# A mixture of experts after a convolution on one core: the fixed blocks of experts 1 to 6 go from 256 to 512 rows

## The chip, the core and the metric

The kernel runs on one core of a Trainium2 chip. Its engines work side by side, each through its own queue in order: TensorE (PE in the profile, its weight loads PEld), VectorE (DVE), ScalarE (ACT), GpSimd (POOL, which issues the indirect gathers and scatters) and SyncE (SP, which issues the other transfers). The metric is the time of one execution in microseconds (us).

## The reference

The input `x` has 8 batches of 3584 rows of 192 numbers. A causal convolution of 7 taps with softmax weights, one set for each of 8 heads of 24 columns, comes first. Then every row is a token of a mixture of 8 experts:

```python
skip_score = x @ w_skip
do_compute = skip_score > 0
xc = x[do_compute]
e_idx = argmax(xc @ w_gate, axis=1)
gate_w = softmax(xc @ w_gate)[arange, e_idx]
for e in range(E):                       # E = 8, D = 192, F = 1024
    mask = e_idx == e
    h = maximum(xc[mask] @ w1[e], 0.0)
    y[mask] = gate_w[mask, None] * (h @ w2[e])
out[do_compute] = xc + y
```

So about half of the 28672 tokens go through one expert each, a product with a 192 x 1024 matrix and one with a 1024 x 192 matrix; the others keep the convolution's result.

## The kernel before

**Two phases.** The first phase convolves batch by batch, stores the result in `out`, routes each token and builds lists of token numbers by expert (`sidx`; `sidxa` for the tokens of the first five batches that chose expert 0 or 1). The second phase works through a list of *blocks*. A block is a group of tokens of one expert; 128 tokens are a *column* of the list (`us` is the block's number of columns, one or two). There are 61 blocks: numbers 0 to 7 (the tail, experts 0 and 1 from `sidxa`, while the first phase ends), 8 to 49 (the fixed sequence: "122" for experts 0 and 1, six blocks of two columns for each of experts 2 to 7), and 50 to 60 (dynamic: whatever is left, expert and column read from a table). `NTAIL` is 8.

**The stages of a block.** `gather` fetches its rows from `out` into a row buffer `y` with one indirect transfer per column, `gather_gates` its gates. `prep` takes the largest absolute value of each row (L779), makes a power of two of it (three small DVE steps), scales the row to f16 on ACT (`yt`, L784), puts the rest that f16 lost beside it with two DVE instructions per column (L789), and transposes it into `m` by a transfer (L792). `up` is the first product: for each group of 128 hidden units five passes of a 128 x 128 weight over the block's rows, into a bank of PSUM (`ph`, 512 columns of f32). With 256 rows a bank holds two groups. ACT takes the positive part in f16 (`hh`, L818), DVE the rest (`hl`, L820), and with that the bank is free. `down` is the second product: for each column 8 times a pass of 384 and one of 192 columns into a bank `po` (L850, L853), and then DVE scales it (`yf`, L830), adds it to the row in two steps (`o`, L836) and POOL scatters it to `out` (L839).

**What sets the order.** Every engine's queue is filled in the order in which the Python code runs. In the loop over blocks at L1087, iteration n writes `up(n+1)`, the gates of n+2, the gathers, then `down(n)`. `weave` runs such a stage, which stops once per bank in `up` (after `hh`, ahead of `hl`) and once per column in `down`, and at each stop it writes one step of background work (`bg`) and PU = 2 or PD = 4 steps of `prep` of a later block. `gather` runs up to AHEAD = 5 blocks ahead, `prep` PREP = 3. The background is `split_weights` of the next expert: 7 loads, 7 DVE reductions of 512 columns (L260), one `partition_all_reduce` on POOL (L266) whose result the next DVE step (`pow2_steps`, L309) needs, then 7 pairs of an ACT and a DVE instruction of 512 columns (L279, L290). It must be over when the next expert's first `up` is written: `background(-1)` writes out what is left of it.

**Banks.** `bank` takes the next PSUM pool in turn. From block 8 on the turn for `ph` is over `ps_h` (3 banks), `ps_h2` (2 banks), `ps_h`; that for `po` over `ps_o` (one bank) and `ps_o2` (two). So every second column's sum goes into the one bank of `ps_o`, and a `ph` bank is used again four, five or six banks later:

```python
def bank(pools):
    pools.append(pools.pop(0))
    return pools[-1]
```

Of the kernel before, what the change touches and what calls it, by code (L numbers as in the profile page):

```python
# [17 lines left out]
P = 128  # L18
# [24 lines left out]
REST = "122"  # L43
# [28 lines left out]
PREP = 3  # L72
PREP0 = 3
# [8 lines left out]
def conv_router_moe(ctx: ExitStack, tc: tile.TileContext, x, weight, w_skip, w_gate, w1, w2, out):  # L82
# [662 lines left out]
    def open_row_buffers():  # L745
        for n in range(DEPTH):
            ybuf.append(wk2.tile([P, 2, D], F32, tag=f"y{n}", bufs=1, name=f"y{n}"))
            gbuf.append(wk2.tile([P, 2], F32, tag=f"g{n}", bufs=1, name=f"g{n}"))
            nc.gpsimd.memset(ybuf[n], 0.0)
            nc.gpsimd.memset(gbuf[n], 0.0)  # L750
# [7 lines left out]

    def gather(k, fixed=True):
        k.y = ybuf[k.n % DEPTH]  # L760
        for u in range(k.us):
            rows_apart(nc.gpsimd.indirect_dma_start(  # L762
                out=k.y[:, u, :], out_offset=None, in_=out[0:k.rows, :],
                in_offset=bass.IndirectOffsetOnAxis(ap=k.si[:, u:u + 1], axis=0),
                bounds_check=k.rows - 1, oob_is_err=False), fixed)

    def gather_gates(k):
        k.g = gbuf[k.n % DEPTH]
        for u in range(k.us):
            nc.gpsimd.indirect_dma_start(  # L770
                out=k.g[:, u:u + 1], out_offset=None, in_=gate_dr[0:k.rows, :],
                in_offset=bass.IndirectOffsetOnAxis(ap=k.si[:, u:u + 1], axis=0),
                bounds_check=k.rows - 1, oob_is_err=False)

    def prep(k):

        am = k.am = wk2.tile([P, 2], F32, tag="yam", bufs=6, name=f"yam{k.n}")
        sc = wk2.tile([P, 2], F32, tag="ysc", bufs=3, name=f"ysc{k.n}")
        nc.vector.tensor_reduce(out=am[:, 0:k.us], in_=k.y[:, 0:k.us], axis=AX.X, op=ALU.max, apply_absolute_value=True)  # L779
        yield  # L780
        yield from pow2_steps(am[:, 0:k.us], sc[:, 0:k.us])
        yt = wk2.tile([P, 2, 2 * D], F16, tag="yt", bufs=3, name=f"yt{k.n}")
        for u in range(k.us):
            nc.scalar.activation(yt[:, u, 0:D], k.y[:, u, :], AF.Copy, scale=sc[:, u:u + 1])  # L784
        yield
        k.m = wk2.tile([P, 3, BLK], F16, tag="m", bufs=MBUF, name=f"m{k.n}")
        for u in range(k.us):
            for (a, b_, o) in ((P, D, D), (0, P, D + 64)):
                nc.vector.scalar_tensor_tensor(out=yt[:, u, o:o + b_ - a], in0=k.y[:, u, a:b_],  # L789
                                               scalar=sc[:, u:u + 1], in1=yt[:, u, a:b_],  # L790
                                               op0=ALU.mult, op1=ALU.subtract)
            nc.sync.dma_start_transpose(out=k.m[:, :, u * P:(u + 1) * P], in_=yt[:, u, :])  # L792
            yield

# [10 lines left out]
    def up(k, wt):  # L805
        k.hh = wk3.tile([P, NF, BLK], F16, tag="hh", bufs=2, name=f"hh{k.n}")
        k.hl = wk3.tile([P, NF, BLK], F16, tag="hl", bufs=2, name=f"hl{k.n}")
# [15 lines left out]
    def down(k, wt, fixed=True):  # L823

        wide = k.n >= NTAIL
        o = wk3.tile([P, 2, D], F32, tag="o", bufs=3, name=f"o{k.n}")
        f2 = wk2.tile([P, 2], F32, tag="yf", name=f"yf{k.n}")

        def scale():
            nc.vector.scalar_tensor_tensor(out=f2[:, 0:k.us], in0=k.am[:, 0:k.us], scalar=winv_of(wt),  # L830
                                           in1=k.g[:, 0:k.us], op0=ALU.mult, op1=ALU.mult)

        def finish_rows(u, *parts):
            base = k.y[:, u, :]
            for part in parts:
                nc.vector.scalar_tensor_tensor(out=o[:, u, :], in0=part, scalar=f2[:, u:u + 1], in1=base,  # L836
                                               op0=ALU.mult, op1=ALU.add)
                base = o[:, u, :]
            rows_apart(nc.gpsimd.indirect_dma_start(  # L839
                out=out[0:k.rows, :], out_offset=bass.IndirectOffsetOnAxis(ap=k.si[:, u:u + 1], axis=0),  # L840
                in_=o[:, u, :], in_offset=None, bounds_check=k.rows - 1, oob_is_err=False), fixed)
# [31 lines left out]
    blocks = []  # L873

    def add_block(si, e=None, l=None, rows=NTOK):
        k = Blk()
        k.n, k.e, k.l, k.si, k.rows, k.us = len(blocks), e, l, si, rows, si.shape[1]
        blocks.append(k)
# [10 lines left out]
    for e in range(E):  # L889
        add_blocks(e, REST if e < NA else "2" * NST,  # L890
# [24 lines left out]
    dynw = {}  # L915
# [10 lines left out]
    for b in range(B):  # L926
        if b == B - 1:
            xeven.close()
            wk2 = ctx.enter_context(tc.tile_pool(name="wk2", bufs=2))
            open_row_buffers()  # L930
# [121 lines left out]
    dynw = {}  # L1052
# [25 lines left out]

    routes.append(whole_route(B - 1))
# [7 lines left out]
    for n in range(NBLK):  # L1087
# [3 lines left out]
        if n == NTAIL:  # L1091
# [3 lines left out]
            wk4 = ctx.enter_context(tc.tile_pool(name="wk4", bufs=1))  # L1095
            ph_pools.append(ctx.enter_context(tc.tile_pool(name="ps_h2", bufs=2, space=PSUM)))
# [8 lines left out]
        m = n + PREP + 1  # L1105
        if m < NBLK and blocks[m].l is not None:
            l = blocks[m].l
            dynw[l] = wk4.tile([P, WW], F16, tag="wd", bufs=5, name=f"wd{l}")
            bg.append(dyn_weights(l, dynw[l]))
        while prepped < min(n + PREP + 1, gathered):  # L1110
# [11 lines left out]
        while gathered < min(n + AHEAD + 1, ready):  # L1122
# [8 lines left out]
        if n >= NTAIL + 8 and n % 2 == 0 and (n - NTAIL - 8) // 2 < NDYN:  # L1131
            dyn_lists((n - NTAIL - 8) // 2)
# [4 lines left out]
    with tc.If(left > 0):  # L1137
        fill = wk4.tile([P, E * SPAN // P], I32, tag="fill", bufs=1, name="fill")
# [9 lines left out]
        for e in range(E):  # L1148
            first = nc.values_load(lo_hi[0:1, e:e + 1], min_val=0, max_val=NTOK // BLK)
            last = nc.values_load(lo_hi[0:1, E + e:E + e + 1], min_val=0, max_val=NTOK // BLK)  # L1150
            with tc.For_i(first, last, 1) as i:
                k = Blk()
                k.n, k.rows, k.us = NBLK + e * DEPTH, NTOK, 2
# [3 lines left out]
                wt = wk4.tile([P, WW], F16, tag="wd", bufs=5, name=f"wf{e}")  # L1157
# [32 lines left out]
```

## Time and profile before

| | |
|---|---|
| three runs | 714.67, 716.00, 716.28 us; median 716.0 |
| the profiled execution | 714.31 us, its span 712.5 us, mean granted TensorE clock 0.969 |
| PE, PEld, DVE, ACT, POOL busy | 93%, 75%, 81%, 45%, 56% of the span |
| PE instructions | 5768 matmuls, as many weight loads |
| `up` of two columns | 40 passes of 256 columns, 4.37 us |
| fixed blocks of two columns | one every 8.29 us from 313 us to the end of the fixed sequence |

Times in the profile are us from the start of the span, each row an instruction or several alike that follow each other (x40): start, length, engine, line, operation, output <- input. A length is that of the whole instruction; the next one may start before it ends, so what an instruction takes from its engine is the distance to the next start. POOL's rows are the making of a transfer's list, not the transfer. "Idle before" and "waits" name the engine or transfer whose signal came last.

### The profile page before, as it was taken

The numbers are of one execution on the slowest core, as the hardware profiler recorded it, in microseconds if no ns is written. First come the engines' busy times: TensorE is split into PE (matmuls) and PEld (weight loads), VectorE is DVE, ScalarE is ACT, GpSimd is POOL, SyncE is SP. The second block draws the span as 40 slices with busy tenths as digits, with TensorE's granted clock in tenths as the row PEclk, the third lists the DMA queues.
The fourth block names the chain that finished last, engine by engine and source line by source line (L and its number), as shares of the span: only waits on it lengthen the run. The fifth ranks groups of instructions, "written<-read, shape, count | busy, mean of one in ns | idle before, by whom it ended". The sixth has DMA issues, their size and how long they took to land.

```text
span 712.5 us, 16377 instructions
## 1 busy us (share of the span) xinstructions
PE 666.1 (93%) x5768; PEld 534.8 (75%) x5768; DVE 580.2 (81%) x1533; ACT 319.6 (45%) x654; POOL 399.5 (56%) x435
## 2 busy tenths in 40 slices
PE   4979699699999889999999999999999999999994
PEld 4646476466678889888888888888888888888883
DVE  4428679589899987998998998998998987777762
ACT  3646376367673223354363453543543533343321
POOL 4401020110750556777777777777777777777642
PEclk8998799799999999999999999999999999999997
DMA  7699889989495355466467357367465536999950
GB/s 227 204 263 291 235 235 287 249 202 268 114 224 180 84 128 130 110 163 150 130 171 171 89 168 181 89 159 170 125 181 118 166 84 182 268 315 267 314 171 12
DMA packets 158037, 129.59 MB, mean 182 GB/s; under 512 B 63238, under 2 KB 144904, under 8 KB 157946
## 3 DMA queue, kind: packets, MB, share of 16 engines
q1 hardware_dynamic: 143226, 106.59, 55.5%
q0 software_dynamic: 14720, 21.86, 12.3%
q8 instruction: 47, 0.77, 0.5%
q14 instruction: 44, 0.36, 0.2%
HBM read 69.76 MB, written 48.15 MB: 165 GB/s over the span
## 4 chain that ended last, share of the span: by engine, by line
PE 71%; DVE 13%; DMA 6%; issue 3%; SPq 2%; ACT 2%; POOL 2%; POOLq 0%; DVEq 0%; ACTq 0%
PE ph L815 33%; PE po L850 18%; PE po L853 9%; DMA out_dram<-ys 5%; PE pc L337 3%; DVE ob L617 3%; PE po L865 2%; PE tp L423 2%; SPq L390 2%; DVE oa L606 1%; DVE hl L820 1%; PE pp L350 1%; DMA raw<-in_moe_w_dram 1%; DVE oa L611 1%; DVE yt L789 1%
## 5 line engine op out<-in xcount | busy, mean ns | idle before, releaser
L818 ACT ACTIVATE hh<-ph 128x512 f16<-128x512 f32 x230 | 133.1, 590 | 226.5 <-PE ph L815 210.8
L815 PE MATMUL ph<-m,wt 128*128 128x256 f16 (+1 forms) x2000 | 220.4, 268 | 4.2 <-DVE hl L820 3.1
L815 PEld LDWEIGHTS <-wt 128*128 128x128 f16 x2000 | 188.7, 98 | 27.2 <-issue 5.0
L850 PE MATMUL po<-wt,hh 128*128 128x384 f16 x656 | 167.5, 326 | 0.0
L820 DVE SCALAR_TENSOR_TENSOR hl<-ph,hh 128x512 f16<-128x512 f32 x230 | 155.4, 685 | 11.1 <-ACT hh L818 9.9
L853 PE MATMUL po<-wt,hl 128*128 128x192 f16 x656 | 147.5, 246 | 0.0
L850 PEld LDWEIGHTS <-hh 128*128 128x128 f16 x808 | 78.3, 98 | 39.7
L770 POOL DMA_INDIRECT g<-gate_dr,sidx x82 | 87.4, 1066 | 25.0 <-issue 24.1
L839 POOL DMA_INDIRECT out_dram<-o,sidx x82 | 84.6, 1031 | 25.1 <-issue 6.4
L762 POOL DMA_INDIRECT y<-out_dram,sidx x82 | 83.9, 1023 | 25.3 <-issue 18.6
L853 PEld LDWEIGHTS <-hl 128*128 128x128 f16 x808 | 79.1, 98 | 10.2
L337 PE MATMUL pc<-xs,toep 128*120 128x360 f32 x224 | 82.1, 491 | 0.0
L836 DVE SCALAR_TENSOR_TENSOR o<-po,yf,y 128x192 f32<-128x192 f32 x115 | 47.3, 415 | 42.3 <-PE po L850 34.6
L784 ACT ACTIVATE yt<-y,ysc 128x192 f16<-128x192 f32 x115 | 46.4, 447 | 62.5 <-DVE ysc L314 52.9
L339 ACT COPY ys<-pc 120x720 f32<-120x720 f32 x56 | 42.6, 761 | 58.1 <-PE pc L337 33.5
L789 DVE SCALAR_TENSOR_TENSOR yt<-y,ysc,yt 128x64 f16<-128x64 f32 x230 | 58.3, 313 | 1.8 <-ACT yt L784 1.7
L337 PEld LDWEIGHTS pc<-xs,toep 128*120 128x120 f32 x224 | 38.3, 191 | 15.0 <-issue 2.0
L423 PE MATMUL tp<-ident,ys 120*128 120x120 f32 x240 | 33.1, 283 | 15.4 <-ACT ya L424 15.4
L260 DVE TENSOR_REDUCE am<-raw 128x1 f32<-128x512 f32 x56 | 37.8, 677 | 11.8 <-DMA raw<-in_moe_w_dram 11.5
L423 PEld LDWEIGHTS tp<-ident,ys 120*128 120x128 f32 x240 | 28.0, 149 | 25.7 <-ACT ya L424 17.7
L290 DVE SCALAR_TENSOR_TENSOR wt<-raw,ar,wt 128x512 f16<-128x512 f32 x56 | 41.8, 747 | 5.7 <-ACT wt L279 5.7
L836 DVE SCALAR_TENSOR_TENSOR o<-po,yf,o 128x192 f32<-128x192 f32 x101 | 42.2, 418 | 3.6
(197 smaller groups left out, 958.2 us busy)
## 6 DMA issues: line engine op xcount, KB each, us to landing
wd<-wscr SPq DMA_DIRECT2D x44, 449.0 KB
xs<-in_x_dram SPq DMA_DIRECT2D x6, 2688.0 KB
out_dram<-ys SPq DMA_DIRECT2D x6, 2610.0 KB
wscr<-wt SPq DMA_DIRECT2D x84, 128.0 KB
raw<-in_moe_w_dram SPq DMA_DIRECT2D x32, 192.0 KB
raw<-in_moe_w_dram SPq DMA_DIRECT2D x8, 512.0 KB
raw<-in_moe_w_dram SPq DMA_DIRECT2D x16, 256.0 KB
wscr<-wt SPq DMA_DIRECT2D x14, 256.0 KB
```

Source lines behind the costliest of these rows:

```text
L337: nc.tensor.matmul(pc[0:R, i, 0:n * G], toep[:, h, :], xs[:, c0 + n * i:c0 + n * i + n, h * G:(h + 1) * G], start=True, stop=True)
L423: nc.tensor.transpose(tp[:, u, :], src, ident[0:R, 0:R])
L762: rows_apart(nc.gpsimd.indirect_dma_start(out=k.y[:, u, :], out_offset=None, in_=out[0:k.rows, :], in_offset=bass.IndirectOffsetOnAxis(ap= ...
L770: nc.gpsimd.indirect_dma_start(out=k.g[:, u:u + 1], out_offset=None, in_=gate_dr[0:k.rows, :], in_offset=bass.IndirectOffsetOnAxis(ap=k.si ...
L789: nc.vector.scalar_tensor_tensor(out=yt[:, u, o:o + b_ - a], in0=k.y[:, u, a:b_], scalar=sc[:, u:u + 1], in1=yt[:, u, a:b_], op0=ALU.mult, ...
L815: nc.tensor.matmul(ph[:, f - f0, :], wt[:, o + f * P:o + (f + 1) * P], k.m[:, m, 0:w], start=(n == 0), stop=(n == len(seq) - 1))
L818: nc.scalar.activation(hh, ph, AF.Relu)
L820: nc.vector.scalar_tensor_tensor(out=k.hl[:, f0:f0 + fs, 0:w], in0=ph, scalar=0.0, in1=hh, op0=ALU.max, op1=ALU.subtract)
L836: nc.vector.scalar_tensor_tensor(out=o[:, u, :], in0=part, scalar=f2[:, u:u + 1], in1=base, op0=ALU.mult, op1=ALU.add)
L839: rows_apart(nc.gpsimd.indirect_dma_start(out=out[0:k.rows, :], out_offset=bass.IndirectOffsetOnAxis(ap=k.si[:, u:u + 1], axis=0), in_=o[: ...
L850: nc.tensor.matmul(po, k.hh[:, f, u * P:(u + 1) * P], w2[:, f], start=(f == 0), stop=(f == NF - 1))
L853: nc.tensor.matmul(po[:, 1], k.hl[:, f, u * P:(u + 1) * P], w2[:, f, 0], start=False, stop=False)
```

## The change

The fixed sequence becomes "122" for expert 0, "14" for expert 1, "444" for experts 2 to 6 and six blocks of two for expert 7: 26 blocks in the place of 42, 45 in all. Blocks 12 to 27 have four columns. In `up` of such a block a pass streams 512 columns and a `ph` bank holds one group of hidden units, so that it stops eight times. Row buffers belong to pairs of columns (a block of four takes two; four more of them are opened at block 8 and set to zero by DVE, where POOL does it for the first seven). `prep` does the reduction, the ACT step and the rest for each pair, and the three small steps once for all. The `hh` and `hl` of wide blocks lie in the end of the memory that the dynamic experts' weights use later. `near` limits gathers to three wide blocks ahead and `prep` to two, and holds wide blocks back until block 8. The dynamic blocks' lists are fetched at every block from 14 on, not at every second one from 16 on.

```diff
-REST = "122"
+REST = ("122", "14")
+DEPTH4 = 11
+AHEAD4 = 3
+PREP4 = 2
+LISTS = 6
+NWD = 5
 def prep(k):
-        nc.vector.tensor_reduce(out=am[:, 0:k.us], in_=k.y[:, 0:k.us], axis=AX.X, op=ALU.max, apply_absolute_value=True)
-        yield
+        for i, us, n in pairs(k):
+            nc.vector.tensor_reduce(out=am[:, us], in_=k.y[i][:, 0:n], axis=AX.X, op=ALU.max, apply_absolute_value=True)
+            yield
         yield from pow2_steps(am[:, 0:k.us], sc[:, 0:k.us])
...
+        for i, us, n in pairs(k):
+            yt = wk2.tile([P, 2, 2 * D], F16, tag="yt", bufs=3, name=f"yt{k.n}_{i}")
+            for u in range(n):
+                nc.scalar.activation(yt[:, u, 0:D], k.y[i][:, u, :], AF.Copy, scale=sc[:, 2 * i + u:2 * i + u + 1])
             yield
+            for u in range(n):
...
+                nc.sync.dma_start_transpose(out=k.m[:, :, v * P:(v + 1) * P], in_=yt[:, u, :])
+                yield
 def up(k, wt):
+        if k.us == 4:
+            k.hh, k.hl = hwide[k.n % 2]
     for e in range(E):
-        add_blocks(e, REST if e < NA else "2" * NST,
+        add_blocks(e, REST[e] if e < NA else "2" * NST if e == E - 1 else "4" * (NST // 2),
+    def near(i, n, small, large):
+        if blocks[i].us == 4 and n < NTAIL:
+            return False
+        return i <= n + small and sum(k.us == 4 for k in blocks[n + 1:i + 1]) <= large
...
+            open_row_buffers(wk4, nc.vector, range(DEPTH, DEPTH4))
...
-        while prepped < min(n + PREP + 1, gathered):
+        while prepped < gathered and near(prepped, n, PREP, PREP4):
...
-        while gathered < min(n + AHEAD + 1, ready):
+        while gathered < ready and near(gathered, n, AHEAD, AHEAD4):
             gather(blocks[gathered])
...
-        if n >= NTAIL + 8 and n % 2 == 0 and (n - NTAIL - 8) // 2 < NDYN:
-            dyn_lists((n - NTAIL - 8) // 2)
+        if 0 <= n - NTAIL - LISTS < NDYN:
+            while tables:
+                tail_slot()
+            dyn_lists(n - NTAIL - LISTS)
```

**What moves on the engines.** On PE 640 matmuls and 640 weight loads go. The three places that the prediction speaks of follow, a row per instruction (or several alike, x2), with its line, operation, output <- input; a bracket names the engines or transfer counters for which the row is written to wait (a wait that an earlier row of the queue already made is not written again).

POOL around block 8 before: gates of blocks 9 and 10 (`g`), rows of 12 and 13 (`y`), the scatters of blocks 7 and 8, the reduction over partitions for expert 2's scales (ISA), and the gates of block 11.

```order
L770 DMA g_1890<-gate_dr,sidx 128x1 x2
L762 DMA y_1901<-out_dram,sidx 128x192 x2
L839 DMA out_dram<-o_3706,sidxa 17920x192
L770 DMA g_1894<-gate_dr,sidx 128x1 x2
L762 DMA y_1905<-out_dram,sidx 128x192 x2
L839 DMA out_dram<-o_3854,sidx 28672x192
L266 ISA sc_3938<-ar_3936 128x2
L770 DMA g_1898<-gate_dr,sidx 128x1
```

and after:

```order
L865 DMA out_dram<-o_0_3736,sidxa 17920x192
L783 DMA g_1894<-gate_dr,sidx 128x1 x2
L775 DMA y_1901<-out_dram,sidx 128x192 x2
L775 DMA y_1905<-out_dram,sidx 128x192 x2
L775 DMA y_3749<-out_dram,sidx 128x192 x2
L775 DMA y_3753<-out_dram,sidx 128x192 x2
L865 DMA out_dram<-o_0_3904,sidx 28672x192
L272 ISA sc_3964<-ar_3962 128x2
L783 DMA g_1898<-gate_dr,sidx 128x1
```

The rows of block 12 moved from ahead of block 7's scatter to behind the gates of block 10, and with blocks 12 and 13 twice as wide eight gathers stand in one piece ahead of the scatter of block 8 and the reduction.

PE at the end of a block's second column before (block 19, the last of expert 2 there; `hh`, `hl` are the stationary operands):

```order
L853 LDWEIGHTS hl19_5114
L853 MATMUL po19_1_5372<-wt2_3486,hl19_5114 128x192
L850 LDWEIGHTS hh19_5113
L850 MATMUL po19_1_5372<-wt2_3486,hh19_5113 128x384
L815 LDWEIGHTS wt3_4542 [waits DMAHW5_49]
L815 MATMUL ph21_0_5397<-m21_5174,wt3_4542 128x256 [waits DMAHW4_49]
```

and after, in `down` of block 14 (its `hh` and `hl` lie in `wdall`):

```order
L879 LDWEIGHTS wdall_3765
L879 MATMUL po14_1_4919<-wt2_3486,wdall_3765 128x192
L876 LDWEIGHTS wdall_3765
L876 MATMUL po14_1_4919<-wt2_3486,wdall_3765 128x384
L876 LDWEIGHTS wdall_3765 [waits DVE_49]
L876 MATMUL po14_2_4945<-wt2_3486,wdall_3765 128x384 [waits PE_49]
```

Before, the first product of block 21 followed a second column; now the block's third column follows, and it takes the bank of `ps_o` that the first column filled, so its first weight load waits for DVE.

DVE where an expert changes, before (end of block 18, then block 20, the first of expert 3; `yam`, `ysc` and `yt` belong to the `prep` of block 22):

```order
L836 SCALAR_TENSOR_TENSOR o18_5207<-po18_1_5232,yf18_5208,y4_1897 128x192 [waits PE_49]
L836 SCALAR_TENSOR_TENSOR o18_5207<-po18_1_5232,yf18_5208,o18_5207 128x192 [waits DVE_49]
L779 TENSOR_REDUCE yam22_5279<-y1_1885 128x2 [waits DMASW3_49,DMASW2_49]
L309 TENSOR_SCALAR yam22_5279<-yam22_5279 128x2 [waits DVE_49]
L820 SCALAR_TENSOR_TENSOR hl20_5266<-ph20_0_5267,hh20_5265 128x512 [waits Activation_49]
L311 TENSOR_SCALAR yam22_5279<-yam22_5279 128x2 [waits DVE_49]
L314 TENSOR_SCALAR ysc22_5280<-yam22_5279 128x2 [waits DVE_49]
L820 SCALAR_TENSOR_TENSOR hl20_5266<-ph20_2_5284,hh20_5265 128x512 [waits Activation_49]
L789 SCALAR_TENSOR_TENSOR yt22_5298<-y1_1885,ysc22_5280,yt22_5298 128x64 [waits DMAHW1_49,DMAHW0_49,Activation_49]
```

and after (end of block 14, then block 16, the first of expert 3; the `prep` is that of block 17, and the `hl` of block 16 is written to `wdall`):

```order
L862 SCALAR_TENSOR_TENSOR o14_2_4966<-po14_3_4972,yf14_4889,o14_2_4966 128x192 [waits DVE_49]
L296 SCALAR_TENSOR_TENSOR wt3_4540<-raw3_4548,ar3_4794,wt3_4540 128x512 [waits Activation_49] x3
L793 TENSOR_REDUCE yam17_5028<-y4_1897 128x2 [waits DMASW5_49,DMASW4_49]
L793 TENSOR_REDUCE yam17_5028<-y5_1901 128x2 [waits DMASW7_49,DMASW6_49]
L842 SCALAR_TENSOR_TENSOR wdall_3765<-ph16_0_5021,wdall_3765 128x512 [waits Activation_49]
L315 TENSOR_SCALAR yam17_5028<-yam17_5028 128x4 [waits DVE_49]
L317 TENSOR_SCALAR yam17_5028<-yam17_5028 128x4 [waits DVE_49]
L842 SCALAR_TENSOR_TENSOR wdall_3765<-ph16_1_5033,wdall_3765 128x512 [waits Activation_49]
L320 TENSOR_SCALAR ysc17_5029<-yam17_5028 128x4 [waits DVE_49]
L808 SCALAR_TENSOR_TENSOR yt17_0_5052<-y4_1897,ysc17_5029,yt17_0_5052 128x64 [waits DMAHW7_49,DMAHW6_49,Activation_49]
L808 SCALAR_TENSOR_TENSOR yt17_0_5052<-y4_1897,ysc17_5029,yt17_0_5052 128x128
L842 SCALAR_TENSOR_TENSOR wdall_3765<-ph16_2_5043,wdall_3765 128x512 [waits PE_49]
```

What is left of `split_weights` (three L296 instructions) now stands ahead of block 16's first `hl`, two reductions stand there in the place of one, and the small step that makes `ysc` stands right ahead of the first `yt` that needs ACT's result from it, without an `hl` between.

106 lines of the change are left out of this document (62 added, 44 removed).

## The prediction

> **What bounds the kernel now.** I read the page first, then its span in windows, the waits of PE, the chain of waits, and the timelines of DVE and POOL. The page's busy shares and slices (each digit a fortieth of the span):
>
> ```profile
> PE 666.1 (93%) x5768; PEld 534.8 (75%) x5768; DVE 580.2 (81%) x1533; ACT 319.6 (45%) x654; POOL 399.5 (56%) x435
> PE   4979699699999889999999999999999999999994
> DVE  4428679589899987998998998998998987777762
> PEclk8998799799999999999999999999999999999997
> ```
>
> From the sixteenth slice on PE is full and its clock too; DVE stands at eight or nine tenths until expert 7. The windows of that stretch, busy time with the number of instructions:
>
> ```profile
> core 0: us, PE busy (x) PEld busy (x) DVE busy (x) ACT busy (x) POOL busy (x), PEclk, DMA share, GB/s
> 300.00:360.00 60.00, 60.00 (x544) 49.66 (x542) 56.13 (x162) 28.09 (x56) 46.39 (x46) 1.00 0.57 138
> 600.00:660.00 60.00, 60.00 (x523) 49.07 (x521) 45.37 (x123) 21.69 (x43) 46.27 (x46) 1.00 1.05 279
> ```
>
> PE is the bound, but DVE has only 3.9 us of every 60 left while weights are split. POOL is closer still: 46 instructions, with 0.3 us ahead of each (rows below), make 46.4 + 13.8 = 60.2. The waits of PE from 240 us on, in total, times, longest:
>
> ```profile
> PE ph L815 <- DVE hl L820: 1.8, 1, 1.8
> ```
>
> That one is ahead of the stretch (at 251 us). The chain of waits, merged (start, length), gives the passes:
>
> ```profile
> 292.67 4.37 PE ph L815 x40
> 300.96 2.23 PE ph L815 x40
> 307.11 4.37 PE ph L815 x40
> 313.44 4.37 PE ph L815 x40
> ...
> 404.59 4.37 PE ph L815 x40
> 412.88 4.37 PE ph L815 x40
> ```
>
> Forty passes of 256 columns take 4.37 us, 109.25 ns each; forty of 128 take 2.23, 55.75 each. Two blocks start 8.29 us apart, so a column's second product takes (8.29 - 4.37) / 2 = 1.96.
>
> **The gain.** The two lengths differ by 53.5 ns for 128 columns, so 2.25 ns of each pass do not depend on its columns. 640 passes go: 640 x 2.25 ns = 1.4 us. A wide `up` takes 40 x (55.75 + 3 x 53.5) = 8.65 us, 1.08 per bank. The weight loads that go cost nothing now: they lie beside passes (PEld busy 49.66 of 60, PE never idle). That is all that PE gains; the rest is what the engines behind it must do with blocks twice as long and with no more banks.
>
> **The rule on longer passes.** The Trainium skill (TensorE: Matmul & The Clock Gate, section Back-to-back issue gap) says of streams of load and pass that 128 columns take about 81 ns and 512 about 131. The rows above disagree for 128 columns, 55.75; for 512 no row here shows it, and by the rule the sum would be a large gain; it is the second rival.
>
> **The start of wide blocks.** POOL's timeline around block 8:
>
> ```profile
> 288.16 0.99 POOL L762 DMA_INDIRECT y<-out_dram,sidx  x1 [0.30 <-ACT hh L818]
> ...
> 290.77 1.03 POOL L839 DMA_INDIRECT out_dram<-o,sidxa  x1 [0.30 <-issue]
> 292.10 1.04 POOL L770 DMA_INDIRECT g<-gate_dr,sidx  x1 [0.31 <-issue]
> ...
> 299.61 0.38 POOL L266 PARTITION_ALL_REDUCE sc<-ar  x1 [1.24 <-DVE more L1047]
> ...
> 301.73 1.00 POOL L762 DMA_INDIRECT y<-out_dram,sidx  x1 [0.30 <-issue]
> 303.03 0.99 POOL L762 DMA_INDIRECT y<-out_dram,sidx  x1 [0.30 <-issue]
> ```
>
> A gather takes 1.30 us of the queue, a scatter or gate 1.33. Now block 7's scatter starts at 288.16; two gates, eight gathers and block 8's scatter follow (1.33 + 2.66 + 10.4 + 1.33), so the reduction starts at 303.9 and ends at 304.3, not at 300.0. DVE's timeline shows who needs it:
>
> ```profile
> 301.66 0.16 DVE L309 TENSOR_SCALAR sc<-sc 128x2 f32<-128x2 f32 x1
> ...
> 303.75 0.54 DVE L779 TENSOR_REDUCE yam<-y 128x2 f32<-128x384 f32 x1
> 304.33 0.21 DVE L309 TENSOR_SCALAR yam<-yam 128x2 f32<-128x2 f32 x1
> ...
> 306.06 0.74 DVE L290 SCALAR_TENSOR_TENSOR wt<-raw,ar,wt 128x512 f16<-128x512 f32 x1
> 306.72 1.00 DVE L789 SCALAR_TENSOR_TENSOR yt<-y,ysc,yt 128x64 f16<-128x64 f32 x4
> 307.63 0.22 DVE L830 SCALAR_TENSOR_TENSOR yf<-yam,wt,g 128x2 f32<-128x2 f32 x1
> 307.94 0.42 DVE L836 SCALAR_TENSOR_TENSOR o<-po,yf,y 128x192 f32<-128x192 f32 x1
> 308.39 0.42 DVE L836 SCALAR_TENSOR_TENSOR o<-po,yf,o 128x192 f32<-128x192 f32 x1
> 308.73 0.74 DVE L290 SCALAR_TENSOR_TENSOR wt<-raw,ar,wt 128x512 f16<-128x512 f32 x1
> ...
> 311.49 0.68 DVE L820 SCALAR_TENSOR_TENSOR hl<-ph,hh 128x512 f16<-128x512 f32 x1
> 312.09 0.74 DVE L290 SCALAR_TENSOR_TENSOR wt<-raw,ar,wt 128x512 f16<-128x512 f32 x1
> ```
>
> From start to start: `hl` 0.60, a weight's rest 0.66, a reduction of `y` 0.58, four `yt` 0.91, `yf` 0.31, the two `o` of a column 0.79. The step at 301.66 now waits until 304.35. (The four memsets that DVE takes over cost between nothing and POOL's length; that and the doubled reduction of block 12 lie inside this wait.) From that step to the end of block 12's first `hl` DVE took 312.09 - 301.66 = 10.43 us. After the change that stretch has the second halves of the `prep` of blocks 12 and 13, 0.91 + 0.58 + 0.91, no `prep` of block 14 (0.58 + 0.08 less), and one new wait: `ysc` stands right ahead of the `yt` that goes through ACT. The price of that wait is in three rows of DVE and ACT:
>
> ```profile
> 401.05 0.17 DVE L314 TENSOR_SCALAR ysc<-yam 128x2 int32<-128x2 int32 x1
> ...
> 401.26 0.80 ACT L784 ACTIVATE yt<-y,ysc 128x192 f16<-128x192 f32 x2 [2.13 <-DVE ysc L314]
> ...
> 401.80 1.00 DVE L789 SCALAR_TENSOR_TENSOR yt<-y,ysc,yt 128x64 f16<-128x64 f32 x4
> ```
>
> 0.75 from start to start; an `hl` fills it now, and unfilled it leaves 0.67 idle. So block 12's first `hl` ends at 304.35 + 10.43 + 2.40 - 0.66 + 0.67 = 317.2, its second 1.26 later, 318.45. PE had started this `up` at 307.11. By the turn of the pools its sixth bank is the one that the second `hl` empties (four back), so banks six to eight run from 318.45 to 321.7, where 307.11 + 8.65 = 315.8 was due: 5.9 us lost. Part of it comes earlier, in `down` of block 10, whose second column needs the bank of block 9's second `o`; it is inside the 5.9. The gathers of block 15, which POOL reaches some 10 us late, land while PE is delayed, so they cost nothing; without the delay they would be late next.
>
> **Every change of expert.** Within a wide block the third column takes the bank of the first, so DVE must have its two `o` done 2 x 1.96 us after `up` ends. Count from the start of the `up` at which expert 3's maxima end (block 15; `down` of 14): the last `o` of block 13 0.1 + 0.79, a reduction of weights, two of `y` (1.16), eight `hl` (4.8), another reduction of weights, three small steps and the wait on ACT (0.35 + 0.67), eight `yt` (1.84), the scales (0.5), one rest of weights (0.66), two `yf` (0.62), two `o` (0.79). A weight's reduction is priced by this group of DVE (mean ns of one), less the 0.08 that an `hl` row shows over its step:
>
> ```profile
> L260 DVE TENSOR_REDUCE am<-raw 128x1 f32<-128x512 f32 x35 | 23.7, 677 | 0.2
> ```
>
> Sum 0.89 + 0.6 + 1.16 + 4.8 + 0.6 + 1.02 + 1.84 + 0.5 + 0.66 + 0.62 + 0.79 = 13.5, against 8.65 + 3.92 = 12.57: PE waits 0.9. Then the next block begins at 17.4 with three rests of weights (1.98) and both reductions ahead of its first `hl`; DVE, at 18.3 with the last `o`, reaches the end of the third `hl` at 18.3 + 1.98 + 1.16 + 1.8 + 0.35 + 0.67 + 0.45 = 24.7, and the seventh bank, due at 17.4 + 6 x 1.08 = 23.9, waits 0.8. So 1.7 at each of four changes (2 to 3 up to 5 to 6), and about 1 at expert 6, where the `prep` of a block of two comes on top (1.9 more) without the scales: 7.8 us. Bounds: nothing, if DVE's order leaves the 0.9 and 0.8 as slack; 14, if each of the 15 blocks of experts 2 to 6 lost 0.9. I take 7.8, since it is nearest to DVE's 3.9 us of 60, which is 1.1 in a wide block's 16.5.
>
> **The clock.** The windows ahead of the stretch show what a wait of PE costs beside itself:
>
> ```profile
> core 0: us, PE busy (x), PEclk, DMA share, GB/s
> 248.10:251.50 3.40, 2.82 (x28) 1.00 0.41 87
> 251.30:254.70 3.40, 1.59 (x16) 1.00 0.77 187
> 254.70:258.10 3.40, 3.40 (x24) 0.50 0.35 95
> ```
>
> 0.58 us idle in 3.4 left the clock alone; 1.8 idle were followed by 3.4 us at half clock, a loss of 1.7. PE now waits 3 us and more in `up` of block 12: 1.7 us once, 0 to 3.4 as bounds; the waits of 0.9 are nearer to the 0.58 and cost nothing. The Trainium skill (TensorE: Matmul & The Clock Gate, Part 1: The HAM clock gate) halves the clock after an idle window of about 3.4 us. The trace differs, with 1.8 us of idle time; by the page alone this term could be nothing and the sum 1.7 lower.
>
> **No cost.** The three small steps saved per wide block give DVE 0.3 us, counted above. SP has as many transposes and weight transfers; the dynamic lists move earlier, and no wide block needs them. POOL has as many instructions. The dynamic weights' loads wait for the last wide block, several blocks ahead of use. The end (blocks of two, then dynamic) stays as it is.
>
> **Sum.** 714.3 - 1.4 + 5.9 + 7.8 + 1.7 = 728.3. That is against the profiled execution (714.31 with what lies around its span of 712.5); the median of the runs shown is 1.7 higher and their spread 1.6. I say 729.
>
> **Rivals.** First: DVE is not late. Its waits are spread, and if the stretch to block 12's second `hl` were 5.9 us shorter and the sums at the changes 0.9, PE would keep only its gain: 714.3 - 1.4 = 712.9, faster. For it speaks that PE never waited on DVE in the whole stretch; against it that the same sums leave DVE 1.1 us per wide block on average while a bank must be back after 1.96. Second: a pass of 512 takes far less than two of 256 (the page's rule above). Even then a wide block holds twelve POOL instructions of 1.3 us and more, 15.9 against 16.5, so at most 16 x 0.6 us: 704. Third: only the start is late, the changes fit: 714.3 - 1.4 + 5.9 + 0 to 1.7 = 718.8 to 720.5. For it: the 0.9 and 0.8 are differences of long sums. Fourth: every change of expert halves the clock too: five times 1.7 on top, 737. For it: two waits of 0.9 fall near each other; against: the window with 0.58.
>
> **Chances.** Forecast with its own range 723 to 734: 0.62. Only the start: 0.12. The clock at every change, or more waits of that kind: 0.12. DVE not late: 0.09. Passes cheaper than rows say: 0.01. A net within 0.2% either way, which is about what a measurement of this kernel can tell from no change: 0.04. So faster 0.10, same 0.04, slower 0.86. The range 718 to 740 leaves out the three last cases and little more.
>
> **What would show it.** Right: after 300 us PE's waits name DVE `hl` ahead of `ph` (some 4 us around 315) and DVE `o` ahead of `po`, in groups of one or two per expert; the reduction over partitions starts near 304; a window near 318 has half clock; passes of 512 columns lie 216 ns apart. Wrong: no waits of PE in the wide blocks, or waits for transfers (`m`, `y`), which I priced at nothing, or waits in all of them.

## The result and the profile after

The changed kernel takes 732.04 us (median of 4 runs, 728.88 to 734.8) against 715.34 us for the kernel before (median of 4, 713.56 to 716.28): a ratio on record of 1.0241, 95% interval 1.0211 to 1.0270 (the quotient of the two medians is 1.0233; below it differs from the recorded ratio by up to 0.3%). The ratios leave out executions in a slow state: one of e3_ph5 (1389.52 us) and, with e12_start2, one of each kernel. The forecast was 729, with a range of 718 to 740. The profiled execution took 734.49 us, its span 732.8; it is one of the slower two of the four.

The page of the profiled execution, the lines that answer to those shown of before (busy time and share, then tenths in forty slices):

```profile
PE 666.5 (91%) x5128; PEld 469.5 (64%) x5128; DVE 573.4 (78%) x1493; ACT 319.4 (44%) x654; POOL 396.8 (54%) x435
PE   4979599598998899889999999999998999999995
DVE  4328589589899988996996997987978887777763
PEclk8998799799999999999999999999999999999998
```

PE's busy time is the same, 666.5 us for 666.1: one longer pass in the place of two shorter ones costs nearly what those did. DVE has less to do than before and is still what PE waits for, as the windows (same stretches as before) and PE's waits from 240 to 660 us show (total, times, longest):

```profile
300.00:360.00 60.00, 53.98 (x365) 31.98 (x363) 51.69 (x141) 24.91 (x50) 46.39 (x47) 1.00 0.54 135
600.00:660.00 60.00, 60.00 (x525) 49.38 (x524) 45.38 (x124) 22.34 (x44) 43.76 (x43) 1.00 0.82 225
PE po L876 <- DVE o L862: 8.1, 10, 2.4
PE ph L837 <- DVE wdall L842: 5.2, 7, 1.6
PE inv L595 <- DVE ob L623: 2.3, 3, 1.0
PE ph L837 <- DVE hl L842: 1.8, 1, 1.8
PE ph L837 <- DMA m<-yt: 1.6, 1, 1.6
```

In the wide blocks `hh` and `hl` lie in the tile `wdall`, so the second wait is that on `hl`. The two waits named `inv` and `hl` lie ahead of 300 us. The other three are new and make 14.9 us in all: 5.5 in three waits at the start, 9.4 in fifteen behind it. PE's timeline shows where they stand. Behind the start each of the four changes of expert has a wait of 0.36 on `o` and one of 0.7 on `hl` (372.58 and 383.81, then 425.25 and 436.49). A block ahead of each change stands one more on `o`, of 0.3 to 0.6 (355.57, 408.25), and one of 2.43 stands at the end of expert 6 (times in us from the span's start; the bracket is the idle time ahead of the row and what ended it):

```profile
309.87 0.34 PE L876 MATMUL po<-wt,hh 128*128 128x384 f16 x1 [2.27 <-DVE o L862]
313.58 2.75 PE L837 MATMUL ph<-m,wt 128*128 128x512 f16 x12 [1.57 <-DMA m<-yt]
320.75 3.40 PE L837 MATMUL ph<-m,wt 128*128 128x512 f16 x15 [1.62 <-DVE wdall L842]
325.95 8.80 PE L837 MATMUL ph<-m,wt 128*128 128x512 f16 x40
...
355.57 0.34 PE L876 MATMUL po<-wt,wdall 128*128 128x384 f16 x1 [0.43 <-DVE o L862]
372.58 0.34 PE L876 MATMUL po<-wt,wdall 128*128 128x384 f16 x1 [0.36 <-DVE o L862]
383.81 2.32 PE L837 MATMUL ph<-m,wt 128*128 128x512 f16 x10 [0.67 <-DVE wdall L842]
398.59 3.40 PE L837 MATMUL ph<-m,wt 128*128 128x512 f16 x15 [0.30 <-DVE wdall L842]
402.50 1.24 PE L837 MATMUL ph<-m,wt 128*128 128x512 f16 x5 [0.51 <-DVE wdall L842]
408.25 0.34 PE L876 MATMUL po<-wt,wdall 128*128 128x384 f16 x1 [0.59 <-DVE o L862]
425.25 0.34 PE L876 MATMUL po<-wt,wdall 128*128 128x384 f16 x1 [0.36 <-DVE o L862]
436.49 2.32 PE L837 MATMUL ph<-m,wt 128*128 128x512 f16 x10 [0.67 <-DVE wdall L842]
...
564.83 0.34 PE L876 MATMUL po<-wt,wdall 128*128 128x384 f16 x1 [2.43 <-DVE o L862]
586.91 1.26 PE L837 MATMUL ph<-m,wt 128*128 128x256 f16 x10
```

Forty passes of 512 columns take 8.80 us with the last one's tail, some 216 ns each. A wide block that waits for nothing lasts 16.47 us from one `up` to the next (the one of 325.95 is followed by one at 342.42); two blocks of before last 2 x 8.29 = 16.57.

**A measure that leaves out the early noise.** The first 300 us differ between executions, in a part that the change hardly touches: the last one-column `up` starts between 300.62 and 307.13 us in the profiles of e2 to e10. So the runs below are also compared by the *stretch* from the last one-column `up` (at 302.95 in this profile) to the first `up` of expert 7 (586.91): 284.0 us here. The same stretch takes 269.4 us in the kernel before (from 300.80 to 570.16) and holds one second product of two columns (3.9 us) more there, because blocks of four lag by more columns; 265.4 is therefore what before takes for the same work. 284.0 - 265.4 = 18.6 us are lost. From 325.95 to 586.91 there are 260.96 us for 15 blocks that need 15 x 16.47 = 247.1: 13.9 of the loss lie behind the start.

### The profile page after: what moved, and what is told of

It reads as the page before. It is cut to its first block, busy times and chain, and to the rows that moved or that the text cites. A ratio compares the mean times of both kernels' runs of the same rounds, so it can differ in the third digit from the quotient of the medians.

```text
span 732.8 us, 14932 instructions
## 1 busy us (share of the span) xinstructions
PE 666.5 (91%) x5128; PEld 469.5 (64%) x5128; DVE 573.4 (78%) x1493; ACT 319.4 (44%) x654; POOL 396.8 (54%) x435
## 5 line engine op out<-in xcount | busy, mean ns | idle before, releaser
L837 PE MATMUL ph<-m,wt 128*128 128x512 f16 (+2 forms) x1360 | 217.5, 316 | 11.1 <-DVE wdall L842 5.2
L837 PEld LDWEIGHTS <-wt 128*128 128x128 f16 x1360 | 125.9, 98 | 92.6 <-issue 14.6
L876 PE MATMUL po<-wt,wdall 128*128 128x384 f16 x512 | 131.4, 329 | 5.9 <-DVE o L862 5.8
L840 ACT ACTIVATE wdall<-ph 128x512 f16<-128x512 f32 x128 | 73.6, 590 | 131.9 <-PE ph L837 131.7
L879 PE MATMUL po<-wt,wdall 128*128 128x192 f16 x512 | 115.9, 248 | 0.0
L840 ACT ACTIVATE hh<-ph 128x512 f16<-128x512 f32 x102 | 59.8, 592 | 121.8 <-PE ph L837 120.5
L775 POOL DMA_INDIRECT y<-out_dram,sidx x82 | 82.3, 1004 | 25.3 <-issue 19.8
L842 DVE SCALAR_TENSOR_TENSOR wdall<-ph,wdall 128x512 f16<-128x512 f32 x128 | 85.1, 681 | 0.6 <-ACT wdall L840 0.6
L842 DVE SCALAR_TENSOR_TENSOR hl<-ph,hh 128x512 f16<-128x512 f32 x102 | 69.8, 689 | 9.1 <-ACT hh L840 7.9
L876 PEld LDWEIGHTS <-wdall 128*128 128x128 f16 x512 | 49.9, 99 | 36.1 <-DVE o L862 8.9
L879 PEld LDWEIGHTS <-wdall 128*128 128x128 f16 x512 | 50.5, 99 | 8.6 <-issue 0.3
L266 DVE TENSOR_REDUCE am<-raw 128x1 f32<-128x512 f32 x56 | 37.8, 677 | 14.6 <-DMA raw<-in_moe_w_dram 14.3
L429 PEld LDWEIGHTS tp<-ident,ys 120*128 120x128 f32 x240 | 28.1, 149 | 28.3 <-ACT ya L430 20.1
```

The source lines that it names most:

```text
L429: nc.tensor.transpose(tp[:, u, :], src, ident[0:R, 0:R])
L775: rows_apart(nc.gpsimd.indirect_dma_start(out=row(k, u), out_offset=None, in_=out[0:k.rows, :], in_offset=bass.IndirectOffsetOnAxis(ap=k.s ...
L837: nc.tensor.matmul(ph[:, f - f0, :], wt[:, o + f * P:o + (f + 1) * P], k.m[:, m, 0:w], start=(n == 0), stop=(n == len(seq) - 1))
L840: nc.scalar.activation(hh, ph, AF.Relu)
L842: nc.vector.scalar_tensor_tensor(out=k.hl[:, f0:f0 + fs, 0:w], in0=ph, scalar=0.0, in1=hh, op0=ALU.max, op1=ALU.subtract)
L876: nc.tensor.matmul(po, k.hh[:, f, u * P:(u + 1) * P], w2[:, f], start=(f == 0), stop=(f == NF - 1))
```

## The experiments

Theory A: DVE gives banks back late inside wide blocks, by its order and the few banks. Rivals: what came with the change costs (M); DVE's sheer amount of work (B); `y` reaches DVE late through POOL's queue (Q). All ratios are to the kernel before on the same chip.

| run | edit to the changed kernel | ratio (95%) | stretch, us | PE's waits from 300 to 590 us |
|---|---|---|---|---|
| changed kernel | none | 1.0241 (1.0211 to 1.0270) | 284.0 | 14.9 |
| e1_narrow | blocks of two | 1.0007 (0.9991 to 1.0023) | - | 0.8 |
| e2_po3 | `po` round three banks | 1.0182 (1.0157 to 1.0206) | 277.0 | 10.9 |
| e3_ph5 | `ph` round five banks | 1.0269 (1.0243 to 1.0295) | 284.1 | 14.6 |
| e4_poph | both turns | 1.0140 (1.0115 to 1.0165) | 276.5 | 9.1 |
| e5_start | one wide gather per iteration | 1.0252 (1.0223 to 1.0281) | 285.2 | 15.6 |
| e6_pu1poph | e4, slower `prep` | 1.0064 (1.0039 to 1.0090) | 271.4 | 6.0 |
| e7_gfpoph | e4, `y` ahead of gates | 1.0032 (1.0009 to 1.0055) | 268.9 | 4.0 |
| e8_gfall | e5, e6 and e7 | 1.0077 (1.0050 to 1.0103) | 271.6 | 5.0 |
| e9_gf | `y` ahead of gates alone | 1.0176 (1.0147 to 1.0205) | 277.2 | 11.3 |
| e10_ms | e7, zeroing by ACT | 1.0040 (1.0021 to 1.0059) | 268.7 | 4.0 |

**Blocks of two with all the rest of the change (e1_narrow).**

```diff
-REST = ("122", "14")
+REST = ("122", "122")
-        ... "2" * NST if e == E - 1 else "4" * (NST // 2)
+        ... "2" * NST
```

> All blocks of experts 0 to 7 have two or one column again; the four more row buffers with their memsets on DVE, the early dynamic lists, the shared tile for dynamic weights and the prep code by pairs stay. Theory A (the loss is DVE giving banks back late inside wide blocks): as the kernel before, 713 to 717 us, and PE waits for nothing between 300 and 660 us. Rival M (what came with the change costs: memsets, lists moved earlier, weights in one tile): over 719 us, with waits of PE on m, y or weights.

1.0007 (718.86 us, where the kernel before took 718.66 on that chip), and two waits of 0.4 us, on `o` at 310.19 and on `hl` at 320.14. The buffers, lists and the shared tile cost nothing that the ratio shows and less than 1 us of PE's waits: the loss comes with the wide blocks. Rival M is out.

**The turns of the banks (e2_po3, e3_ph5, e4_poph).**

```diff
             po_pools.append(ctx.enter_context(tc.tile_pool(name="ps_o2", bufs=2, space=PSUM)))
+            po_pools.append(po_pools[-1])                       # e2, e4
-            ph_pools.append(ps_h)
+            ph_pools[:] = [ps_h] * 3 + ph_pools[-1:] * 2        # e3, e4
```

> The changed kernel, but po goes round its three banks (ps_o, ps_o2, ps_o2), so that a column's bank is that of the third column back and not of the second. Theory A (a bank comes back late; DVE has time to spare in the second product, 22.6 us in 31 waits on PE): most of the 8.1 us that PE waits on o go; DVE is then as late as before at the next up, so some of it comes back as waits on hl: 3 to 8 us off, 724 to 729. Rival B (DVE's work is the limit, not the bank's distance): what goes from the waits on o comes back on hl, 732 as the changed kernel.

> The changed kernel, but ph goes round its five banks in the turn 3 + 2, so that each bank comes back five banks later (now four, five or six). Theory A: the 0.7 us waits of up on hl, once per expert, and some 1 us of the one at the start go; the waits on o stay: 2 to 4 us off, 728 to 730. Rival B: 732, the waits on o grow by as much.

> Both turns, of po and of ph, at once. Theory A: a late bank is late for one of the two pools only while the other bridges it, so both together take more than the sum of each: 8 to 11 us off, 721 to 724; what stays is the start at 310 to 323 us, 4 us or more. Rival B (DVE's work is the limit): 730 to 732. If the sum is just that of e2 and e3, the two waits are independent.

The turn of `po` alone took 7.0 us off the stretch and 0.6% off the ratio; the waits on `o` went from 8.1 to 1.9, and 2 us came back on `hl` and `m`. The turn of `ph` alone gave nothing: the waits on `hl` went from 5.2 to 0.7 us, and those on `o` rose from 8.1 to 11.9. That is rival B's answer for this one edit: where DVE doesn't get ahead, a bank more at one place moves the wait to the next. Both turns took 7.5 off, only 0.5 more than `po` alone. So A's "more than the sum" hardly shows, and the 7.5 is less than the 8 to 11 that I expected. What may have held it back stands in the waits of DVE, in the changed kernel and in e4, from 326 to 586 us:

```profile
DVE yam L793 <- DMA y<-out_dram,sidx: 6.2, 5, 2.0
```

```profile
DVE yam L793 <- DMA y<-out_dram,sidx: 14.2, 6, 3.4
```

The first row is the changed kernel, the second e4: the sooner PE gets through, the longer DVE waits for gathered rows. The runs on POOL's order, below, put that to the test.

**The start (e5_start).**

```diff
             gather(blocks[gathered])
             gathered += 1
+            if blocks[gathered - 1].us == 4:
+                break
```

> The changed kernel, but an iteration gathers at most one wide block: iteration 8 issues four gathers of y and not eight, the second four come an iteration later. Theory A (the reduction over partitions stands on POOL behind eight gathers, and with it DVE's whole queue): it starts some 5.2 us earlier, at 300.6 after the drift, and of the 6.3 us that PE loses between 305 and 326 us (waits of 2.27 on o, 1.57 on m, 1.62 on hl) 3 to 5 go; the rest of the trace as it was: ratio to the kernel before 1.017 to 1.021 where the changed kernel has 1.024. Rival S: DVE is late there by its own work (two halves of prep and the wait on ACT), the reduction is off its path: within 1 us of the changed kernel.

1.0252, as rival S says. In e5 the reduction starts at 302.17, which is 1.0 us behind the last one-column `up` (301.16 there), where it was 2.9 in the changed kernel: 1.9 earlier and not 5.2, since POOL now waits for DVE ahead of it:

```profile
302.17 0.36 POOL L272 PARTITION_ALL_REDUCE sc<-ar  x1 [2.93 <-DVE more L1080]
```

And DVE comes to the step that uses it at 304.91, without a wait, 3.75 us behind that `up` as against 3.84. The changed kernel's rows show why that was no gain:

```profile
305.84 0.33 POOL L272 PARTITION_ALL_REDUCE sc<-ar  x1
306.79 0.16 DVE L315 TENSOR_SCALAR sc<-sc 128x2 f32<-128x2 f32 x1
```

Even there the reduction had ended (305.84 + 0.33) 0.6 us before DVE reached the step. DVE was late by its own work, in which these rows (the four buffers' zeroing, each 0.42 us from start to start) stand ahead; they are from e7, the same code:

```profile
289.35 0.38 DVE L755 MEMSET y<- 128x384 f32 x1
...
290.60 0.38 DVE L755 MEMSET y<- 128x384 f32 x1
```

And in e5 the second four gathers, now an iteration later, came too late for `prep` (DVE waits 0.53 and 2.18 us for `y` at 308 to 311), so that PE waits 4.28 us in one piece at 321.85, with the clock at half for 6.8 us around it. This makes the start 5.3 us longer than in the changed kernel (28.3 us from the last one-column `up` to the `up` of block 13, for 23.0). The wait of 2.43 at the end of expert 6 and the half clock behind it, on the other hand, are not there; why is not shown. So the ratio came out like the changed kernel's by two differences that nearly cancel; what e5 does show is that the earlier reduction didn't bring DVE's step forward.

**The order within a block (e6_pu1poph).**

```diff
-            weave(up(blocks[n + 1], weights_of(n + 1)), ahead, PU)
+            weave(up(blocks[n + 1], weights_of(n + 1)), ahead, 1 if blocks[n + 1].us == 4 else PU)
```

> The two turns of e4, and a wide up takes one step of prep per bank in place of two, so that part of the prep lies in the second product, where DVE waits for PE (9.1 us in ten waits in e4, 22.6 in the changed kernel). Theory A (what is left is DVE's order within a block): the waits on hl of 0.3 to 0.6 us (3.6 in all in e4) go, only the start stays: 2 to 4 us under e4, ratio 1.009 to 1.012. Rival Q (POOL's queue is the next limit: 12 DMAs of 1.3 us per block of 16.5 us, y arrives late in e4, 14.2 us of waits of DVE): a later prep delays m, PE then waits on m, ratio 1.014 or above.

1.0064, 5.1 us less stretch than e4, more than expected. PE's waits on `hl` fell from 3.6 to 0.3, and the wait of DVE on ACT inside `prep` went too (8.0 us in 14 times before, 0.6 once here), since a bank's `hl` now lies between; in its place `hl` waits for ACT's `hh`, 6.4 us in 22 times. The three waits on `m` of 0.4 to 0.6 us behind the start are new: rival Q's sign, at a small price.

**Gathers ahead of gates (e7_gfpoph with the turns, e9_gf alone).**

```diff
-        if 2 < n + 2 < NBLK:
+        if 2 < n + 2 < NBLK and n < NTAIL:
             gather_gates(blocks[n + 2])
         ...                                   # the loop that gathers y
+        if n >= NTAIL and n + 2 < NBLK:
+            gather_gates(blocks[n + 2])
         weave(down(k, weights_of(n)), ahead, PD)
```

> The two turns of e4, and from block 8 on an iteration gathers y ahead of the gates, which are needed a block later. Rival Q (y is late by POOL's queue): gathers land 5.3 us earlier, DVE's 14.2 us of waits on y go, and with them most of the 3.6 us of PE's waits on hl; the start gains too (2.66 us earlier gathers, though the reduction's place stays): 3 to 5 us under e4, ratio 1.007 to 1.010. Theory A (DVE's waits on y lie in time that it has to spare): the waits on y go and PE's waits stay, ratio 1.012 to 1.015.

> The changed kernel with one edit: from block 8 on an iteration gathers y ahead of the gates; the turns of po and ph stay as the change has them. Theory Q (the blocks after the start lose because y reaches DVE late through POOL's queue): DVE's waits on y (6.2 us in five) go, and most of the 13.9 us that the blocks from 326 us on lose; ratio 1.004 to 1.010, stretch from the last one-column up to expert 7 of 270 to 276 us where the changed kernel has 284.0 and e7 268.9. Theory AQ (late y is one part, the banks' distance another, and only both together let PE through): 1.013 to 1.019, 277 to 281 us, with PE's waits on o of 0.4 and on hl of 0.7 still there.

With the turns, PE waits for nothing from 326 us to the end of the wide blocks, though DVE has the same work to do: there rival B is out. All of its waits in e7 from 300 to 590 us:

```profile
PE ph L837 <- DMA m<-yt: 2.6, 1, 2.6
PE po L876 <- DVE o L862: 1.4, 1, 1.4
```

Alone, the same edit took 6.8 us off the stretch, and DVE's five waits on `y` went. The turns took 7.5, both edits 15.1. Each of these three holds the same 1.7 us, the half clock at the end of expert 6, which none of e4, e7 and e9 has; without it they are 5.1, 5.8 and 13.4. So 2.5 us come off only with both edits, and theory AQ stands. The ratios (0.65%, 1.01% and 2.09% off) point the same way but can't tell this from a plain sum: each has an interval of about 0.25% to either side. A look at POOL in the changed kernel and in e7 shows what moved; a block's `y` and gates are four rows each:

```profile
434.05 1.05 POOL L783 DMA_INDIRECT g<-gate_dr,sidx  x1 [0.30 <-issue]
...
439.58 0.99 POOL L775 DMA_INDIRECT y<-out_dram,sidx  x1 [0.30 <-ACT wdall L840]
...
443.49 1.00 POOL L775 DMA_INDIRECT y<-out_dram,sidx  x1 [0.31 <-issue]
```

```profile
444.53 1.14 POOL L775 DMA_INDIRECT y<-out_dram,sidx  x1 [0.30 <-ACT yt L803]
...
449.91 1.00 POOL L783 DMA_INDIRECT g<-gate_dr,sidx  x1 [0.30 <-issue]
```

In the first, `y` starts 5.5 us after the iteration's first gate; DVE, which had done one half of that `prep`'s maxima at 447.47, waits 1.16 us for the other half and starts it at 449.18; the `hl` of the next `up` stand behind it in DVE's queue. In the second `y` goes first.

What e9 leaves in the expert changes is DVE's own lateness: one wait of 0.4 on `o` and one of 0.7 on `hl` per expert. The second wait on `o` of each expert, which in the changed kernel came some 11 us after DVE's wait for `y` (397.39, then 408.25), is gone. Its four waits on `o` stand at 374.07, 424.87, 475.75 and 526.62, 50.9 us apart where 3 x 16.47 = 49.4 are needed: 1.5 us per expert. In the changed kernel the same waits (372.58 to 528.19) are 51.9 apart: 2.5 us, so the late rows make 1.0 of it.

**All edits (e8_gfall).** The diffs of e5, e6 and e7 together.

> All four edits at once: both turns, one step of prep per bank of a wide up, one wide block gathered per iteration, gathers ahead of gates. If the list of causes is complete, PE waits less than 3 us between 300 and 600 us and the passes saved (1.4 us) show: ratio 0.999 to 1.004. If DVE's or POOL's work is what bounds wide blocks: 1.007 or more.

1.0077, worse than e7 and in the range of the other theory; PE waits 5.0 us, not less than 3. Its waits behind the start are gone but for 0.8 us, so the list of causes holds there. But the start is as long as in e7 (1.4 on `o`, 2.8 on `m`), and this time its waits halved the clock for one window (0.64 and 0.85 in the windows from 318.2 and 321.6). With the right order of POOL the slower `prep` and the later gathers add nothing: e7 has no wait at all behind the start.

**The start once more (e10_ms, e11_e1n, e12_start2).**

```diff
-            open_row_buffers(wk4, nc.vector, range(DEPTH, DEPTH4))
+            open_row_buffers(wk4, None, range(DEPTH, DEPTH4))
 ...
+            if engine is None:
+                nc.scalar.activation(flat, ident..., AF.Copy, scale=0.0)   # y; g likewise
```

> e7, and the four wide row buffers are zeroed by ACT and not by DVE (1.8 us of DVE between 289 and 291). Theory S (at the start DVE is late by its own work, which has no gap from 286 to 326 us in e7): the waits of PE there, 1.4 on o and 2.6 on m, shrink by 1.5 to 2 us in all: ratio 1.000 to 1.002 where e7 has 1.003. Rival T (m is late through SP and the gathers, not through DVE): the wait on m stays 2.6.

The waits at the start stayed at 4.0 in all (1.1 on `o`, 1.7 on `m`, 1.25 on `hl`), and the waits of DVE from 286 to 328 us say why:

```profile
DVE sc L315 <- POOL sc L272: 1.2, 1, 1.2
```

With the zeroing gone, DVE comes early enough to wait for the reduction, which still stands behind eight gathers. Its step then lies 3.18 us behind the last one-column `up`, 0.4 earlier than in e7 (3.57) and not 1.7. The two delays are of like length and hide each other: e5 took one away, e10 the other, and neither brought the start to an earlier end (block 12 starts 1.25 us earlier in e10 than in e7, then waits 1.25 on `hl`, and block 13 gains 0.1). Both forecasts missed: S's, that the waits shrink, and T's, that the one on `m` stays 2.6.

e11_e1n left expert 1 in blocks of two on top of e7.

> e7, but expert 1's last two blocks stay of two columns and the wide blocks begin with expert 2. DVE has done the table of blocks (the small steps of lines 1040 to 1082) and the memsets by the time that it prepares a wide block. Theory S: the start costs 0 to 2 us instead of 4, ratio 0.998 to 1.002. Rival: the step from blocks of two to blocks of four costs what it costs wherever it stands (two reductions and eight steps of prep between shorter ups), since expert 2's first block also meets the scales of expert 3: ratio 1.003 or above.

It answers nothing: with the wide blocks beginning at another place in the turn of row buffers, two of them take buffers that blocks 10, 11 and 12 still hold, so these blocks work on the wrong rows, and DVE waits 7.27 us for a gather at 317.89. Its ratio, 1.0189, is of the edit's own making.

e12_start2 is e10 with the edit of e5.

> e10 (both turns, y ahead of the gates, row buffers zeroed by ACT) and one wide block gathered per iteration, as in e5. Theory C (the two delays at the start cover each other: with DVE's 1.8 us of zeroing gone it waits 1.24 us for the reduction behind eight gathers, and with the reduction early alone it is late by its own work): DVE's wait of 1.24 on the reduction goes, PE's waits at the start, 4.0 us in e7 and e10, fall to 2 to 2.8; stretch from the last one-column up to expert 7 of 267 to 268 us (268.9 and 268.7 there); ratio 1.000 to 1.003. Rival T (m is late through the gathers and SP's transposes): the waits stay at 4.0, or y is late instead; ratio 1.004 or above.

It ran on a chip on which the kernel before took 839.82 us (median of 17) and this one 836.05: 0.9935, 0.9893 to 0.9976. What bounds there looks like another thing (last section), so the 2 to 2.8 us can't be read from it. DVE's wait of 1.2 us for the reduction is gone, as theory C says; whether both edits together shorten the start on a chip like the others stays open.

## Why the prediction was right, step by step

The direction, the engine that PE waits for and most of the places were right; the total, 729 against 732.04, is 3 us short, and 5.5 short of the profiled execution, of which 2.2 had come before 270 us. Two terms, the start and the clock, came out right in size by luck, since what happened there is not what was forecast.

- **The gain, 1.4 us.** Right: 216 ns per pass of 512 columns as forecast, 16.47 us per wide block for 16.57, 0.1 in each of 16. The Trainium skill (TensorE: Matmul & The Clock Gate, Back-to-back issue gap) gives about 131 ns for 512 columns; the trace's 216 disagrees, and the second rival, which rested on it, is out.
- **The start, 5.9 us.** Right in size, wrong in its cause, so lucky. The block of `up` 12 should have started at 302.95 + 6.15 = 309.1 and started at 313.58, and the next 1.8 us later than due: 6.2 us. The reduction started where it was forecast (305.84, so 303.7 without the 2.2 us by which this execution was late before, for 303.9). But the step that failed is "that step now waits until 304.35": DVE did not wait for the reduction. It reached that step at 306.79 (304.6 without the 2.2), for its own work: the zeroing, which I had put "between nothing and POOL's length" and inside the wait, the second reductions and a wait on ACT (0.52 at 304.61; a second one follows at 313.71). e5 and e10 show that each of the two delays alone is long enough to hold that step: the reduction early, and DVE is late; DVE lighter by the four buffers' zeroing, and it waits 1.2 for the reduction. Also 1.57 of the loss was a wait on `m`, which I had named as a sign against me and priced at nothing; whether DVE or the transfers make `m` late is not shown (in e10 it shrank from e7's 2.6 to 1.7).
- **The changes of expert, 7.8 us.** The term that was mis-sized: 13.9 measured, 1.7 of it the clock, so 12.2. The 1.7 per change that I had worked out from DVE's rows is there, on `o` and on `hl` as forecast, 1.5 in e9, though the two waits themselves are shorter than the 0.9 and 0.8 of the sum (0.4 and 0.7). What failed is the sentence that the late gathers "cost nothing": with gates ahead of `y`, POOL at 15.9 of 16.5 us made `y` late in the blocks behind the start too. With `y` first, e9 gains 6.8 us, 1.7 of them the clock. The end of expert 6, put at about 1, has a wait of 2.43. The bound of 14 for this term held it.
- **The clock, 1.7 us.** Right in size by luck, at another place: not at the start, where the window was forecast, but behind the 2.43 us wait at the end of expert 6, as the last section shows.
- **No cost** for buffers, lists and the shared tile: shown by e1 to within its interval; the zeroing among them does delay DVE at the start of wide blocks.
- **Rivals.** "DVE is not late" fell with PE's first wait. "Only the start" fell with the 13.9. The clock at every change didn't come: waits of 0.4 to 0.7 leave it alone.

The whole, from the profiled execution: 714.3 + 2.2 (late before 270 us) - 1.5 + 6.2 + 13.9 = 735.1, measured 734.49.

## What to carry to other kernels

When blocks grow and the banks do not, check for each pool how long the engine that empties a bank may take before it comes round, and the order of every queue that is nearly full (here POOL, 15.9 of 16.5 us): the turns and the order together took 15.1 of the 18.6 us back, each alone less than half of that. Look for what the late engine itself waits for before you give it more room, and expect that two delays of like length can hide each other, so that taking one away shows nothing. Here that is shown for one step of DVE; that taking both away shortens the start is not.

No version with wide blocks beats the kernel before on a chip like those of the first eleven runs: e7 is the nearest, 0.3% slower. What the longer passes save, 1.5 us, is less than the 4 us of the start that I could not take away.

## What the hardware showed

**Where a wait falls has a say in whether it halves the clock.** In every trace here the clock changes only at borders that lie 3.41 us, or a multiple of it, apart. Cut at these borders, the changed kernel's windows with long waits read (busy time of PE, then the clock granted):

```profile
254.64:258.05 3.41, 1.73 (x17) 1.00 0.86 211
305.84:309.25 3.41, 1.64 (x12) 1.00 0.40 89
561.84:565.25 3.41, 0.98 (x9) 1.00 0.62 164
565.25:568.67 3.42, 3.42 (x17) 0.50 0.84 132
```

1.64 us of busy time kept the clock, 0.98 lost it for the next window, and before the change 1.59 had lost it. No sharp limit lies between: in such windows of before, after and e1 to e10 (240 to 600 us, the window itself at full clock), 1.31 us and less always lost the clock and 1.62 and more never did, but of nine windows with 1.51 to 1.61 four lost it and five kept it. The wait of 1.80 us that ends at 256.31 (253.32 before the change) is in all the profiles of before, after and e1 to e10, and the clock was halved for one window after it in four of these twelve (before, e5, e8, e9); the 2.27 us at 309.87 are cut by a border into 1.66 and 0.6. The Trainium skill (TensorE: Matmul & The Clock Gate, Part 1: The HAM clock gate) says that the window is 3413 ns and free-running, which these borders agree with. Its idle window needs to be only about half idle here.

**A chip on which the engines wait for nothing that the profile shows.** On the chip of e12 both kernels took some 120 us longer. PE's waits there, of e12, over the span:

```profile
PE po L881 <- issue: 26.2, 36, 1.9
PE po L884 <- issue: 22.5, 38, 1.7
PE ph L842 <- issue: 18.1, 29, 2.7
```

66.8 us in which PE waited for nothing that the profile shows; in the profile of the changed kernel no such wait is listed. ACT has 51.8 us of the same kind ahead of its `hh`. There the kernel with 640 fewer passes and loads takes 0.65% less time, 0.9935. That it is the supply of instructions is an argument from these rows, not shown; the kernel before has no profile on that chip.
